# Attention with a mixture of experts on one core: a third buffer and a lead for converted weights, squares in a later place, an earlier column maximum, and row sums that VectorE adds up first

## The chip, the cores and the metric

The kernel runs on one core of one Trainium2 chip. The core has a matrix engine (TensorE, PE in the rows; PEld is its loading of weights), VectorE (DVE), ScalarE (ACT), GpSimd (POOL) and SyncE (SP), each with its own queue of instructions that it takes in order, and 16 DMA engines that all of them share. Engines wait for each other by semaphores. The metric is device time of one execution in microseconds (us).

## What is computed

```python
def _attn_ref(q, k, v, g_q, g_k):              # (4, 12, 448, 64) each
    def rmsnorm(x, g):
        rms = np.sqrt(np.mean(x * x, axis=-1, keepdims=True) + 1e-06)
        return x / rms * g
    q_n, k_n = (rmsnorm(q, g_q), rmsnorm(k, g_k))
    scores = scale * np.matmul(q_n, k_n.transpose(0, 1, 3, 2))
    scores = scores - np.max(scores, axis=-1, keepdims=True)
    attn = np.exp(scores)
    attn = attn / (np.sum(attn, axis=-1, keepdims=True) + 1e-09)
    return np.matmul(attn, v)

x = attention, as (1792, 768)                   # 4 batches of 448 tokens
x = np.maximum(x @ w_in, 0.0) ** 2 @ w_out      # 768 -> 2048 -> 768
logits = x @ phi                                # 32 slots of 8 experts
d = softmax(logits, axis 0); slot_input = d.T @ x
slot_out[e] = np.maximum(slot_input[e] @ w1[e], 0.0) @ w2[e]
out = softmax(logits, axis 1) @ slot_out
```

`w_in` and `w_out` come as 64-bit floats; the kernel turns them into 32-bit floats on the chip.

## The kernel before

The 48 heads are taken as 24 pairs (t = 0 to 23), six to a batch. `attention()` runs over t and, for each t, over the words of `ORDER`, a list written by hand that works on several pairs at once: loads for pair t+6, squares and roots for the norm of pair t+5, transposes of t+3, row maxima of t+2, scores, exponentials, values and sums of t, reciprocals of t-1, the finished pair of t-2. Between the words, a credit counter lets pieces of the expert input layer (`moe_hidden(b)`, for a batch whose six pairs are done) run on TensorE: 16 weight slices a batch, each 18 matmuls `ph<-xh,whl` (six row blocks, three products of high and low parts), then transposes of `gt` in groups of four slices. Up to t = 6 instructions keep the order of the code. Behind that a scheduler places them, by readiness and by their place in the code, so the built order of an engine is not the code's.

The weights reach the expert layer by *conversion units*, 16 of kind `in` and 16 of kind `out`. A unit is fetched (`fetch64`, a DMA of 768 KB that GpSimd issues into a buffer `w64`), then goes through `convert`: two steps on VectorE (`wf<-w`), three on ScalarE (`w<-w`, `wf<-wf`), a third on VectorE; an `in` unit is split and written to DRAM by GpSimd (`whl_s<-w`), from where SyncE loads it again as `whl`; an `out` unit is transposed on TensorE (`pm<-ident,wf`) and multiplied by phi. `CONVERT` says how many units each t starts, at the words `cvt`; `cvx` moves running units on. Units are fetched ahead by `prefetch`, into two buffers (`w64s`) once the expert layer has begun at t = 7, and `ensure` forces a unit that the expert layer needs at once.

What the steps of the argument touch: `square` (line 216: ScalarE squares a loaded `qk`, VectorE sums), `root` (230: at its end GpSimd multiplies four `qk` tiles), `scores` (291: the exponential `p<-pss` frees one of two PSUM buffers `pss`, which the next scores wait for), `values` and `fold` (305, 323), `sums` (327: four or eight matmuls with `ones`, then tiny DMAs `rsh<-sm`), `recip` (348: VectorE waits for `rsh`), `fetch64` to `ensure` (419 to 515), and `moe_hidden` and `dispatch` (545, 628). `dispatch` takes a batch's column maximum over `lsb`, exponentials `et`, and sums with `gn`. After batch 3 the attention's memory is released, and the weights of the eight experts (48 MB) stream in for the rest of the program.

Nearly all instructions are recorded in a helper, so that the rows have line 98 (100 after the change); the tiles tell them apart.

Of the kernel before, what the change touches and what calls it, by code (L numbers as in the profile page):

```python
# [17 lines left out]
def raw(ap):  # L18
# [6 lines left out]
ORDER = (  # L25
    "loadv load s0 mx0 row sq0 cvt out cvx s1 cvx mx1 v0 sq1 cvt cvx s2 cvx mx2 v1 recip cvt root0 cvx "
    "s3 cvx mx3 v2 cvt root1 cvx trans0 trans1 cvx v3 sum root2"
).split()
LEAD = 6

CONVERT = [0, 0, 0, 1, 0, 0, 1, 1, 2, 1, 2, 1, 2, 3, 3, 3, 3, 3, 3, 3]

PACE = 1.12
# [12 lines left out]
def tile_attention_moe_softmoe(  # L46
# [104 lines left out]
    state = {"h": ps_h, "m": ps_m, "n": 0, "cv": True, "w64": 0, "fc": -1, "h0": False, "held": 0}  # L151

# [23 lines left out]
    WF = 3  # L176
    PD = 3
    NSET = 3
# [126 lines left out]
    def values(t, c):  # L305
        if c == 0:
            live[t]["v"] = ps_v.tile([128, 512], F32, tag="v", name=name("pv"))
        ps = live[t]["v"]
        for j in range(2):
            for d in range(0, D, 32):  # L310
                g = 64 * j + d
                mm(
                    ps[g : g + 32, :S],
                    live[t]["vf"][:, j, c, d : d + 32],
                    live[t][f"p{c}"][:, j, :],
                    c == 0,
                    c == NC - 1,
                )
        if c % 2 and t >= FOLD:
            fold(t, c)  # L320


    def fold(t, c):
        p, p1 = live[t][f"p{c - 1}"], live[t][f"p{c}"]
        dve.tensor_tensor(p1, p1, p, ALU.add)

    def sums(t):
        ps = mps()
        folded = t >= FOLD
        for x in (1,) if folded else (0, 1):  # L330
# [5 lines left out]
        tt = att.tile([128, S], F32, tag="t", name=f"t_{t}", bufs=3)  # L336
        act.copy(tt, live[t]["v"][:, :S])
        live[t]["t"] = tt
        sm = att.tile([128, S], F32, tag="sm", name=f"sm_{t}", bufs=1)
        act.copy(sm, ps[:, :S])  # L340
        rsh = att.tile([32, 2, 28], F32, tag="rsh", name=f"rsh_{t}", bufs=2)
        for j in range(2):
            for i in range(2):
                g = 32 * (2 * j + i)
                sp.dma_start(rsh[16 * j : 16 * j + 16, i, :], sm[g : g + 1, :].rearrange("o (r e) -> o r e", r=16))
        live[t]["rsh"] = rsh

    def recip(t):
        rsh = live[t]["rsh"]
        rr = att.tile([32, 28], F32, tag="rr", name=f"rr_{t}", bufs=2)  # L350
        dve.scalar_tensor_tensor(rr, rsh[:, 0, :], TINY, rsh[:, 1, :], ALU.add, ALU.add)
        dve.reciprocal(rr, rr)
# [40 lines left out]

    def attention():
        for t in range(-LEAD, NT + 2):
            pin["on"] = t < PINNED
            todo = CONVERT[t + LEAD] if t + LEAD < len(CONVERT) else 0
# [85 lines left out]
    )  # L483
    fetched = {}
    running = []
# [7 lines left out]
    def convert_step(more, stages):  # L493
# [13 lines left out]
        if not (units or running):  # L507
            state["cv"] = False

    def convert_next():  # L510
# [34 lines left out]
    def moe_hidden(b):  # L545
# [40 lines left out]
        for fc in range(NFC):  # L586
# [39 lines left out]
        yield from dispatch(b, lsb, gn)  # L626

# [360 lines left out]
```

## Time and profile before

| | |
|---|---|
| Three runs, median (range) | 893.85 us (886.15 to 894.22) |
| The profiled execution: its time, and the span of its instructions | 893.53 us, 891.7 us |
| Busy: PE, PEld, DVE, ACT, POOL | 781.2, 471.7, 453.1, 358.9, 136.5 us |
| Mean granted TensorE clock | 0.946 of 2.4 GHz |
| DMA, mean over the span | 202 GB/s, 179.85 MB |

A row of a timeline has the start in us, the duration, engine, line, operation, out<-in, size and count, and in brackets how long the engine stood idle before it and what ended that. A row that counts several instructions has their joint duration. A row of a table by stretches has the stretch, its length, then for each engine busy us and count, the granted clock, the busy share of the DMA engines, and GB/s.

### The profile page before, as it was taken

The numbers are of one execution on the slowest core, as the hardware profiler recorded it, in microseconds if no ns is written. First come the engines' busy times: TensorE is split into PE (matmuls) and PEld (weight loads), VectorE is DVE, ScalarE is ACT, GpSimd is POOL, SyncE is SP. The second block draws the span as 40 slices with busy tenths as digits, with TensorE's granted clock in tenths as the row PEclk, the third lists the DMA queues.
The fourth block names the chain that finished last, engine by engine and source line by source line (L and its number), as shares of the span: only waits on it lengthen the run. The fifth ranks groups of instructions, "written<-read, shape, count | busy, mean of one in ns | idle before, by whom it ended". The sixth has DMA issues, their size and how long they took to land.

```text
span 891.7 us, 13289 instructions
## 1 busy us (share of the span) xinstructions
PE 781.2 (88%) x5162; PEld 471.7 (53%) x5162; DVE 453.1 (51%) x831; ACT 358.9 (40%) x564; POOL 136.5 (15%) x169
## 2 busy tenths in 40 slices
PE   0278888797997898999999999999999998988875
PEld 0134344464564655456666655666666885544433
DVE  4687878585575465456554665443126443210112
ACT  4347666663656354434333342342324432010101
POOL 3312322034142123003020100000000000000000
PEclk9999999699899797999999999999999999797895
DMA  8944667568767465524543421333336973899999
GB/s 268 248 130 143 204 195 214 150 208 290 215 229 255 169 215 173 200 88 124 153 131 109 140 93 47 128 107 113 118 117 245 359 292 136 318 401 348 348 348 295
DMA packets 122655, 179.85 MB, mean 202 GB/s; under 512 B 54624, under 2 KB 99168, under 8 KB 122592
## 3 DMA queue, kind: packets, MB, share of 16 engines
q1 hardware_dynamic: 112256, 129.45, 45.2%
q0 software_dynamic: 10336, 49.55, 16.1%
q8 instruction: 41, 0.67, 0.3%
q14 instruction: 22, 0.18, 0.1%
HBM read 148.73 MB, written 29.97 MB: 200 GB/s over the span
## 4 chain that ended last, share of the span: by engine, by line
PE 64%; DMA 10%; DVE 10%; issue 6%; ACT 5%; SPq 4%; POOL 1%; DVEq 0%; ACTq 0%; POOLq 0%
PE ph L98 23%; PE pm L98 14%; PE pss L98 9%; PE pv L98 7%; PE pe L98 4%; SPq L98 3%; DVE wf L98 3%; PE so_ps L98 3%; DVE nm L98 3%; DMA w<-in_moe_w_out_dram 2%; PE pt L98 2%; DMA w<-in_moe_w_in_dram 2%; DMA qk<-in_k_dram 2%; ACT w L98 1%; DMA w<-in_moe_w_dram 1%
## 5 line engine op out<-in xcount | busy, mean ns | idle before, releaser
L98 PE MATMUL ph<-xh,whl 128*128 128x448 f32 x1152 | 271.9, 379 | 0.7 <-ACT gt L98 0.7
L98 PEld LDWEIGHTS ph<-xh,whl 128*128 128x128 f32 x1152 | 208.2, 189 | 59.0 <-issue 30.2
L98 DVE TENSOR_REDUCE nm<-pss 112x2 f32<-112x896 f32 x96 | 104.2, 1086 | 73.4 <-PE pss L98 73.3
L98 ACT ACTIVATE p<-pss 112x896 f32<-112x896 f32 x96 | 87.9, 915 | 85.2 <-PE pss L98 84.1
L98 PE MATMUL pv<-p,vf 112*32 112x448 f32 x768 | 107.6, 566 | 0.0
L98 ACT ACTIVATE gt<-ph 128x448 f32<-128x448 f32 x64 | 34.8, 543 | 118.7 <-PE ph L98 112.6
L98 ACT ACTIVATE w<-w 128x768 int32<-128x768 f32 (+1 forms) x68 | 59.4, 879 | 36.7 <-DVE wf L98 34.3
L98 POOL TENSOR_TENSOR gt<-gt 128x448 f32<-128x448 f32 x33 | 31.1, 942 | 262.9 <-ACT gt L98 262.8
L98 POOL TENSOR_TENSOR qk<-qk,y 112x512 f32<-112x512 f32 x48 | 54.0, 1152 | 92.6 <-DVE y L98 63.8
L98 PE MATMUL pss<-qh,kh 64*112 64x448 f32 x192 | 46.3, 469 | 21.3 <-ACT p L98 18.5
L98 PE MATMUL pss<-kh,qh 64*112 64x448 f32 x192 | 44.4, 437 | 15.8 <-DVE nm L98 11.2
L98 PE MATMUL pm<-ident,qk 112*128 112x112 f32 x192 | 28.9, 290 | 31.9 <-POOL qk L98 31.0
L98 PEld LDWEIGHTS pss<-qh,kh 64*112 64x112 f32 x192 | 17.4, 175 | 65.0 <-ACT p L98 30.0
L98 PEld LDWEIGHTS pm<-ident,qk 112*128 112x128 f32 x192 | 23.2, 159 | 42.2 <-POOL qk L98 31.7
L98 DVE TENSOR_REDUCE ss<-sq 112x8 f32<-112x512 f32 x48 | 32.1, 674 | 22.1 <-ACT sq L98 21.8
L98 PE MATMUL pm<-ident,gt 128*112 128x128 f32 x256 | 40.9, 286 | 2.1 <-DVE ql L98 1.2
L98 PEld LDWEIGHTS pm<-ident,gt 128*112 128x112 f32 x256 | 28.3, 137 | 27.3 <-issue 14.1
L98 PE MATMUL pss<-ql,kh 64*112 64x448 f32 x192 | 41.5, 382 | 0.0
L98 PE MATMUL pss<-qh,kl 64*112 64x448 f32 x192 | 41.4, 382 | 0.0
L98 DVE SCALAR_TENSOR_TENSOR wf<-wf,w 128x768 f32<-128x768 f32 x32 | 31.9, 997 | 17.0 <-ACT w L98 11.5
L98 PE MATMUL pss<-mr,one 64*112 64x448 f32 x192 | 40.2, 377 | 0.0
L98 DVE TENSOR_TENSOR gt<-gt 128x448 f32<-128x448 f32 x22 | 13.9, 634 | 48.9 <-ACT gt L98 48.9
(145 smaller groups left out, 1010.2 us busy)
## 6 DMA issues: line engine op xcount, KB each, us to landing
w<-in_moe_w_dram SPq DMA_DIRECT2D x48, 1024.0 KB
whl<-whl_s SPq DMA_DIRECT2D x50, 768.0 KB
w<-in_moe_w_in_dram POOLq DMA_DIRECT2D x16, 768.0 KB, 6.5
w<-in_moe_w_out_dram POOLq DMA_DIRECT2D x16, 768.0 KB, 6.5
whl_s<-w POOLq DMA_DIRECT2D x16, 768.0 KB, 4.4
wo_s<-wf POOLq DMA_DIRECT2D x16, 384.0 KB, 6.4
wo<-wo_s SPq DMA_DIRECT2D x6, 1024.0 KB
qk<-in_q_dram SPq DMA_DIRECT2D x48, 112.0 KB
```

What stands on the lines that cost most here:

```text
L98: ins = f(*args, **kw)
```

## The change

1. *Conversion.* A third buffer `w64x`, used in turn with the two; four units ahead are fetched instead of three, three may be held instead of two. From t = 7 a unit starts only when its fetch was recorded at least `READY` = 4 calls of `convert_step` before, both `cvt` and `cvx` can start one, and what was not started stays on the account.
2. *Squares later.* In `ORDER`, `sq0` moves from behind `row` to behind the third scores, `sq1` from behind the first values to behind the fourth scores; `root0` moves ahead of the transposes and `root1` behind them.
3. *Maximum earlier.* In `moe_hidden`, the first part of `dispatch` (its maximum and exponentials) comes ahead of the last group's four transposes.
4. *Sums.* From pair 13 (`FOLD`), VectorE adds all four chunks of exponentials into the first (three adds, before two), and TensorE's four matmuls with `ones` have 224 columns each (before 448). The copy of the values `t` stands ahead of the sums.

```diff
-    "loadv load s0 mx0 row sq0 cvt out cvx s1 cvx mx1 v0 sq1 cvt cvx s2 cvx mx2 v1 recip cvt root0 cvx "
-    "s3 cvx mx3 v2 cvt root1 cvx trans0 trans1 cvx v3 sum root2"
+    "loadv load s0 mx0 row cvt out cvx s1 cvx mx1 v0 cvt cvx s2 cvx sq0 mx2 v1 recip cvt cvx "
+    "s3 cvx sq1 mx3 v2 cvt root0 cvx trans0 trans1 root1 cvx v3 sum root2"
+READY = 4
+    w64x = wst.tile([128, KC, 128, 2], I32, tag="w64x", name="w64x")
-    PD = 3
+    PD = 4
-        if c % 2 and t >= FOLD:
-            fold(t, c)
-    def fold(t, c):
-        p, p1 = live[t][f"p{c - 1}"], live[t][f"p{c}"]
-        dve.tensor_tensor(p1, p1, p, ALU.add)
+        if c and t >= FOLD:
+            p0 = live[t]["p0"]
+            dve.tensor_tensor(p0, p0, live[t][f"p{c}"], ALU.add)
...
-                    c = 2 * i + 1 if folded else 2 * x + i
-                    mm(ps[g : g + 32, :S], ones, live[t][f"p{c}"][:, j, :], folded or x == 0, x == 1)
+                    p = live[t]["p0"][:, j, i * HS : (i + 1) * HS] if folded else live[t][f"p{2 * x + i}"][:, j, :]
+                    mm(ps[g : g + 32, :w], ones, p, folded or x == 0, x == 1)
...
+            todo = max(todo, 0) + (CONVERT[t + LEAD] if t + LEAD < len(CONVERT) else 0)
-                        convert_step(key == "cvt" and todo > 0, 1 if pin["on"] else 2)
-                        todo -= key == "cvt"
+                        if pin["on"]:
+                            convert_step(key == "cvt" and todo > 0, 1)
+                            todo -= key == "cvt"
+                        else:
+                            todo -= convert_step(todo > 0, 2, READY)
...
-            w64 = w64s[state["w64"]]
-            state["w64"] ^= 1
+            w64 = w64s[state["w64"]] if state["w64"] < 2 else w64x
+            state["w64"] = (state["w64"] + 1) % 3
...
-            if key not in fetched and state["held"] < (2 if state["h0"] else 4):
+            if key not in fetched and state["held"] < (3 if state["h0"] else 4):
...
-        if more and units:
+        begin = more and units and not (ready and state["tick"] - since.get(units[0], state["tick"]) < ready)
+        if begin:
...
-        for c in pend:
-            yield c
+        yield next(pend)
+        rest = dispatch(b, lsb, gn)
+        yield next(rest)
+        yield from pend
```

Three places of the built orders follow, before and after. First ScalarE in pair 6: `p_6_1` is the exponential of the pair's second chunk, `sq_12_0` the square of pair 12's q tile. Before:

```order
L98 ACTIVATE p_6_0_1449<-pss_135_1440 112x896
L98 ACTIVATE sq_11_0_1462<-qk_11_0_1255 112x512
L98 ACTIVATE wf_118_1290<-wf_118_1290 128x768
L98 ACTIVATE p_6_1_1480<-pss_139_1471 112x896
L98 ACTIVATE sq_11_1_1491<-qk_11_1_1258 112x512
L98 CAST xh_0_1669<-xf_4_1469 128x448
L98 ACTIVATE sq_12_0_1655<-qk_12_0_1434 112x512
L98 ACTIVATE p_6_2_1508<-pss_144_1499 112x896
L98 ACTIVATE sq_12_1_1768<-qk_12_1_1437 112x512
```

and after:

```order
L100 COPY sm_6_1603<-pm_154_1600 128x448
L100 ACTIVATE w64_131_1394<-w64_131_1394 128x768
L100 ACTIVATE p_7_1_1731<-pss_164_1722 112x896
L100 ACTIVATE sq_12_0_1822<-qk_12_0_1435 112x512
L100 CAST xh_0_1666<-xf_5_1664 128x448
L100 COPY wt_160_1707<-pm_161_1708 128x512
L100 ACTIVATE sq_12_1_1885<-qk_12_1_1438 112x512
```

The squares of pair 12 moved from ahead of the third exponential of pair 6 to behind the second one of pair 7.

Second GpSimd around the four multiplies `qk_12_0` to `qk_13_1`; a `DMA w64..<-in_moe_w` is the fetch of a unit, `whl_s` the write of a split one. Before:

```order
L98 DMA wi_s_90<-wf_191_2019 128x768
L98 DMA whl_s_91<-w64_1_94 128x1536
L98 TENSOR_TENSOR qk_12_0_1434<-qk_12_0_1434,y_13_2149 112x512
L98 TENSOR_TENSOR qk_12_1_1437<-qk_12_1_1437,y_13_2149 112x512
L98 TENSOR_TENSOR qk_13_0_1626<-qk_13_0_1626,y_13_2149 112x512
L98 TENSOR_TENSOR qk_13_1_1629<-qk_13_1_1629,y_13_2149 112x512
L98 DMA w64_1_94<-in_moe_w_in_dram 128x6x256
L98 TENSOR_TENSOR gt_3_1995<-gt_3_1995 128x448
L98 DMA w64_0_93<-in_moe_w_out_dram 128x1536
```

and after:

```order
L100 DMA w64_0_93<-in_moe_w_in_dram 128x6x256
L100 DMA wo_s_92<-wf_174_1819 128x768
L100 TENSOR_TENSOR gt_2_1927<-gt_2_1927 128x448
L100 DMA wi_s_90<-wf_191_2018 128x768
L100 DMA whl_s_91<-w64_1_94 128x1536
L100 DMA w64x_110<-in_moe_w_in_dram 128x6x256
L100 TENSOR_TENSOR gt_3_1997<-gt_3_1997 128x448
L100 DMA w64_1_94<-in_moe_w_out_dram 128x1536
L100 DMA wo_s_92<-wf_192_2024 128x768
L100 DMA whl_s_91<-w64_0_93 128x1536
L100 TENSOR_TENSOR gt_4_2099<-gt_4_2099 128x448
L100 DMA wi_s_90<-wf_194_2042 128x768
```

Unit in 9 is the `w64_1` fetch before and the `w64_0` fetch after. Its fetch, and those of in 10 and out 9, moved from behind the four multiplies to ahead of them; after the change the multiplies follow the last row shown.

Third GpSimd at the start of the program, up to the first multiply `qk_0_0`, which the first transposes on TensorE wait for. Before:

```order
L98 DMA w64_0_93<-in_moe_w_out_dram 128x1536
L98 DMA w64_1_94<-in_moe_w_in_dram 128x6x256
L98 DMA whl_s_91<-w64_1_160 128x1536
L98 DMA w64_6_178<-in_moe_w_out_dram 128x1536
L98 DMA w64_7_180<-in_moe_w_in_dram 128x6x256
L98 DMA whl_s_91<-w64_2_162 128x1536
L98 TENSOR_TENSOR qk_0_0_147<-qk_0_0_147,y_1_210 112x512
```

and after:

```order
L100 DMA w64_4_167<-in_moe_w_out_dram 128x1536
L100 DMA w64_0_93<-in_moe_w_out_dram 128x1536
L100 DMA w64_1_94<-in_moe_w_in_dram 128x6x256
L100 DMA whl_s_91<-w64_1_161 128x1536
L100 DMA w64x_110<-in_moe_w_out_dram 128x1536
L100 DMA w64_7_181<-in_moe_w_in_dram 128x6x256
L100 DMA whl_s_91<-w64_2_163 128x1536
L100 DMA w64_8_191<-in_moe_w_out_dram 128x1536
L100 TENSOR_TENSOR qk_0_0_148<-qk_0_0_148,y_1_213 112x512
```

Two more fetches, `w64x` and `w64_8`, now stand ahead of the first multiply; `w64_7` and `w64_8` take the buffers that the two `whl_s` writes read.

## Rows read from the trace of the kernel before

**Rows 1.** Page, 40 equal slices of 22.3 us: busy tenths of TensorE and VectorE

```profile
PE   0278888797997898999999999999999998988875
DVE  4687878585575465456554665443126443210112
```

**Rows 2.** Table by stretches: length, busy us (count) per engine, clock, DMA share, GB/s

```profile
0.00:25.00 25.00, 0.00 (x0) 0.00 (x0) 11.12 (x28) 9.66 (x13) 8.41 (x18) 1.00 0.91 269
...
150.00:175.00 25.00, 18.58 (x105) 10.71 (x107) 15.34 (x31) 14.97 (x23) 2.17 (x4) 0.73 0.52 158
...
200.00:225.00 25.00, 18.38 (x118) 11.97 (x118) 13.84 (x25) 11.19 (x18) 9.62 (x11) 0.93 0.81 280
225.00:250.00 25.00, 23.85 (x157) 14.40 (x155) 13.87 (x20) 16.33 (x25) 5.30 (x8) 0.94 0.67 202
...
275.00:300.00 25.00, 18.91 (x110) 12.57 (x109) 13.89 (x22) 12.91 (x20) 2.47 (x4) 0.80 0.58 191
284.00:292.00 8.00, 2.89 (x20) 1.93 (x19) 3.64 (x8) 2.79 (x4) 0.42 (x1) 0.85 0.98 341
...
325.00:350.00 25.00, 22.41 (x119) 12.25 (x115) 18.42 (x35) 13.04 (x20) 9.12 (x11) 0.88 0.54 171
350.00:375.00 25.00, 23.55 (x121) 12.69 (x122) 10.57 (x17) 10.02 (x15) 2.55 (x4) 0.84 0.60 213
```

**Rows 3.** Timeline of TensorE, the first row behind each of four stops

```profile
161.73 0.71 PE L98 MATMUL pss<-qh,kh 64*112 64x448 f32 x2 [5.00 <-ACT p L98]
...
223.95 0.71 PE L98 MATMUL pss<-qh,kh 64*112 64x448 f32 x2 [6.62 <-ACT p L98]
...
292.07 0.69 PE L98 MATMUL pm<-ident,wf 128*128 128x128 f32 x2 [4.66 <-DVE gn L98]
...
344.67 0.71 PE L98 MATMUL pss<-qh,kh 64*112 64x448 f32 x2 [2.58 <-DVE nm L98]
```

**Rows 4.** Timelines of ScalarE and VectorE, what they waited for at these stops

```profile
160.25 0.63 ACT L98 ACTIVATE sq<-qk 112x512 f32<-112x512 f32 x1 [6.12 <-DMA qk<-in_q_dram]
...
220.62 0.56 DVE L98 TENSOR_SCALAR wf<-w 128x768 int32<-128x768 int32 x1 [6.63 <-DMA w<-in_moe_w_in_dram]
...
288.12 0.56 DVE L98 TENSOR_SCALAR wf<-w 128x768 int32<-128x768 int32 x1 [2.85 <-DMA w<-in_moe_w_in_dram]
290.19 0.18 DVE L98 SCALAR_TENSOR_TENSOR rr<-rsh 32x28 f32<-32x28 f32 x1 [1.51 <-DMA rsh<-sm]
...
337.89 2.61 DVE L98 TENSOR_SCALAR wf<-w 128x768 int32<-128x768 int32 x2 [1.25 <-DMA w<-in_moe_w_out_dram]
```

**Rows 5.** Waits of VectorE, 150 to 380 us: total, times, longest

```profile
DVE wf L98 <- DMA w<-in_moe_w_in_dram: 14.7, 4, 6.6
```

**Rows 6.** Chain that ended last: ten score matmuls at the low and the full clock

```profile
161.73 2.21 PE pss L98 x10
...
174.38 1.20 PE pss L98 x10
```

**Rows 7.** Timeline of GpSimd ahead of the second stop

```profile
207.01 4.76 POOL L98 TENSOR_TENSOR qk<-qk,y 112x512 f32<-112x512 f32 x4 [3.36 <-issue]
211.72 0.90 POOL L98 DMA_DIRECT2D w<-in_moe_w_in_dram  x1
```

**Rows 8.** Timeline of GpSimd at the start

```profile
22.50 0.84 POOL L98 DMA_DIRECT2D w<-in_moe_w_in_dram  x1 [6.18 <-DMA whl_s<-w]
...
29.09 5.77 POOL L98 TENSOR_TENSOR qk<-qk,y 112x512 f32<-112x512 f32 x4 [5.21 <-issue]
```

**Rows 9.** Page, DMA issues: KB each, median us to landing

```profile
whl_s<-w POOLq DMA_DIRECT2D x16, 768.0 KB, 4.4
```

**Rows 10.** The sums: TensorE's timeline, and VectorE's group, 430 to 680 us

```profile
146.60 1.69 PE L98 MATMUL pm<-p,ones 112*32 112x448 f32 x16
...
L98 DVE TENSOR_TENSOR p<-p,p 112x896 f32<-112x896 f32 x20 | 22.3, 1116 | 23.8 <-PE pv L98 19.5 <-ACT p L98 4.2
```

**Rows 11.** Timeline of TensorE at the end of the expert input layer

```profile
755.07 0.40 PE L98 MATMUL pm<-ident,et 32*112 32x32 f32 x4 [2.15 <-ACT et L98]
```

More of the change, by code (lines that the diff above doesn't have):

```diff
@@ L150, in tile_attention_moe_softmoe @@
     ps_s = tc.alloc_tile_pool(name="ps_s", bufs=2, space=PSUM)
-    state = {"h": ps_h, "m": ps_m, "n": 0, "cv": True, "w64": 0, "fc": -1, "h0": False, "held": 0}
+    state = {"h": ps_h, "m": ps_m, "n": 0, "cv": True, "w64": 0, "fc": -1, "h0": False, "held": 0, "tick": 0}
     def name(s):
@@ L318, in values @@
                 )
-        if c % 2 and t >= FOLD:
-            fold(t, c)
-    def fold(t, c):
-        p, p1 = live[t][f"p{c - 1}"], live[t][f"p{c}"]
-        dve.tensor_tensor(p1, p1, p, ALU.add)
+        if c and t >= FOLD:
+            p0 = live[t]["p0"]
+            dve.tensor_tensor(p0, p0, live[t][f"p{c}"], ALU.add)
+    HS = S // 2
     def sums(t):
@@ L329, in sums @@
         folded = t >= FOLD
+        tt = att.tile([128, S], F32, tag="t", name=f"t_{t}", bufs=3)
+        act.copy(tt, live[t]["v"][:, :S])
+        live[t]["t"] = tt
+        sm = att.tile([128, S], F32, tag="sm", name=f"sm_{t}", bufs=1)
+        rsh = att.tile([32, 2, 28], F32, tag="rsh", name=f"rsh_{t}", bufs=2)
+        live[t]["rsh"] = rsh
+        w = HS if folded else S
         for x in (1,) if folded else (0, 1):
@@ L333, in sums @@
                     g = 32 * (2 * j + i)
-                    c = 2 * i + 1 if folded else 2 * x + i
-                    mm(ps[g : g + 32, :S], ones, live[t][f"p{c}"][:, j, :], folded or x == 0, x == 1)
[L336 to L341, printed above, removed]
+                    p = live[t]["p0"][:, j, i * HS : (i + 1) * HS] if folded else live[t][f"p{2 * x + i}"][:, j, :]
+                    mm(ps[g : g + 32, :w], ones, p, folded or x == 0, x == 1)
+        act.copy(sm[:, :w], ps[:, :w])
         for j in range(2):
@@ L344, in sums @@
                 g = 32 * (2 * j + i)
-                sp.dma_start(rsh[16 * j : 16 * j + 16, i, :], sm[g : g + 1, :].rearrange("o (r e) -> o r e", r=16))
-        live[t]["rsh"] = rsh
+                r = slice(16 * j + 8 * i, 16 * j + 8 * i + 8) if folded else slice(16 * j, 16 * j + 16)
+                src = sm[g : g + 1, :w].rearrange("o (r e) -> o r e", e=28)
+                sp.dma_start(rsh[r, 0 if folded else i, :], src)
     def recip(t):
@@ L350, in recip @@
         rr = att.tile([32, 28], F32, tag="rr", name=f"rr_{t}", bufs=2)
-        dve.scalar_tensor_tensor(rr, rsh[:, 0, :], TINY, rsh[:, 1, :], ALU.add, ALU.add)
+        if t >= FOLD:
+            dve.tensor_scalar(rr, rsh[:, 0, :], TINY, None, ALU.add)
+        else:
+            dve.scalar_tensor_tensor(rr, rsh[:, 0, :], TINY, rsh[:, 1, :], ALU.add, ALU.add)
         dve.reciprocal(rr, rr)
@@ L394, in attention @@
     def attention():
+        todo = 0
         for t in range(-LEAD, NT + 2):
             pin["on"] = t < PINNED
-            todo = CONVERT[t + LEAD] if t + LEAD < len(CONVERT) else 0
+            todo = max(todo, 0) + (CONVERT[t + LEAD] if t + LEAD < len(CONVERT) else 0)
             for key in ORDER:
@@ L400, in attention @@
                     if key == "cvt" or state["h0"]:
-                        convert_step(key == "cvt" and todo > 0, 1 if pin["on"] else 2)
-                        todo -= key == "cvt"
+                        if pin["on"]:
+                            convert_step(key == "cvt" and todo > 0, 1)
+                            todo -= key == "cvt"
+                        else:
+                            todo -= convert_step(todo > 0, 2, READY)
                     continue
@@ L484, in tile_attention_moe_softmoe @@
     fetched = {}
+    since = {}
     running = []
@@ L488, in prefetch, with convert_step @@
         for key in units[:PD]:
-            if key not in fetched and state["held"] < (2 if state["h0"] else 4):
+            if key not in fetched and state["held"] < (3 if state["h0"] else 4):
                 state["held"] += 1
                 fetched[key] = fetch64(*key)
-    def convert_step(more, stages):
+                since[key] = state["tick"]
+    def convert_step(more, stages, ready=0):
+        state["tick"] += 1
+        if ready:
+            prefetch()
         for unit in list(running):
@@ L508, in convert_step @@
             state["cv"] = False
+        return bool(begin)
     def convert_next():
@@ L625, in moe_hidden @@
             state["fc"] += 1
-        yield from dispatch(b, lsb, gn)
+        yield from rest
     def dispatch(b, lsb, gn):
```

## The prediction

> **What bounds the kernel now.** I read the page's slices first. From slice 16 on (about 355 us) to slice 32 TensorE is at 9 tenths or more; before that it is at 7 to 9, with holes [rows 1]. So from 355 us on the time is TensorE's work, and waiting can only be gained back ahead of that, in the tail, or by giving TensorE less to do. The table by stretches shows where the early time goes: between 150 and 375 us TensorE loses 6.4 us of one 25 us stretch, 6.6 of another, 6.1 of a third, and in the same stretches the granted clock is 0.73, 0.93 and 0.80 instead of 1.00 [rows 2]. TensorE's timeline then names four stops: 5.00, 6.62, 4.66 and 2.58 us, together 18.9 us [rows 3]. Behind each the clock is at its lower level of 1.2 GHz for a while. A clock of 0.73 over 25 us means 2 x 0.27 x 25 = 13.5 us at that level; the same sum gives 3.5 and 3.0 us for 200 to 250, 10.0 for 275 to 300, and 6.0 and 8.0 for 325 to 375 [rows 2].
>
> What stood behind the stops is on the other engines [rows 4]. First stop: ScalarE came to a square whose `qk` load was still under way and waited 6.12 us, with the exponential that frees the scores' PSUM buffer queued behind it. Second: VectorE waited 6.63 us for a fetched unit, and ScalarE's next step and exponential came after that. Third: VectorE waited 2.85 us for a unit and 1.51 us for `rsh`, and its `gn` copy, which frees a PSUM buffer, stood behind. Fourth: VectorE waited for a unit again, and the two first steps took 2.61 us. Over 150 to 380 us VectorE's waits for `in` units alone are 14.7 us [rows 5].
>
> **The sum, part by part.** It is made against the profiled execution, 893.53 us (span 891.7); the median of the runs is 893.85, so the two are the same for this purpose.
>
> *Price of the lower clock.* Ten score matmuls take 2.21 us at the low level and 1.20 at the full one [rows 6], so a stretch at the low level wastes 46% of its length if TensorE alone sets the pace. It does not quite: in 150 to 175 us ScalarE is busy 14.97 and VectorE 15.34 of 25 us [rows 2], and with TensorE twice as fast they would have to follow. I take half, 23%; the bounds are 0 and 46%.
>
> *Squares later.* ScalarE's order shows pair 12's squares behind the second exponential of pair 7, almost a whole pair after their load. The first stop goes: 5.0 us, and 23% of its 13.5 us, 3.1. That is 8.1 us (bounds 0 and 11.2). The squares themselves are not fewer. At 0, the stop comes back at another square: the scheduler now puts pair 15's squares ahead of pair 9's first exponential, where they stood behind it.
>
> *Third buffer and lead.* Stops two to four are 6.62 + 4.66 + 2.58 = 13.9 us, their low-clock time 3.5 + 3.0 + 10.0 + 14.0 = 30.5 us, of which 23% is 7.0; in all 20.9 (27.9 at the upper price). How much goes? Before, unit in 9 is fetched behind four multiplies that start at 207.01 and take 4.76 us; the fetch comes at 211.72 and VectorE has it at 220.62 [rows 4, 7]. GpSimd's new order has this fetch and two more ahead of the multiplies. Issued at 207 instead of 211.7 it would be 4.7 us earlier and leave 6.63 - 4.71 = 1.9 us of the wait; the 2.85 and 1.25 us waits are shorter than 4.7 and would go [rows 4]. Against that, the scheduler also begins units earlier: VectorE's order has five, not four, begun between the row maxima of pairs 9 and 10, so part of the lead is spent. And the 1.51 us for `rsh` is not a unit's. I take two thirds of 20.9, **13.9 us**; bounds 0 and 27.9, and below 0 in a rival. The `READY` rule issues nothing.
>
> *Sums.* Sixteen sum instructions take 1.69 us [rows 10], 0.106 each. From pair 13 a pair has eight, 0.85 us; at half the columns 0.42. Eleven pairs save 11 x 0.42 = 4.7 us of TensorE, where it is full; bounds 0 (if loading the `ones` sets the pace) and 4.7. VectorE gets eleven more adds at 1.116 us, 12.3 us, in a part where it is at 3 to 6 tenths [rows 1, 10]; this idle time hides them, and without it they would cost up to 12.3. The last add reads the fourth chunk and no longer writes it, so it need not wait for the value matmuls, which the adds now wait 19.5 us for in twenty [rows 10]; the sums come no later.
>
> *Maximum earlier.* At the end TensorE waits 2.15 us for `et` [rows 11]. The maximum and exponential now run beside the last group's transposes: 2.0 us (bounds 0 and 2.15). For batches 0 to 2 other matmuls hid it.
>
> *Start.* Two more fetches stand ahead of the first multiply. `w64_8` needs the buffer that the second `whl_s` write reads. That write is issued at about 23.3, behind the fetch at 22.50; with 4.4 us to land (median) `w64_8` goes out near 28, and with the 6.2 us that the first write was waited for, near 29.5; half a microsecond later come the multiplies, which began at 29.09 [rows 8, 9]. So 0 to 1 us from the queue. DMA moves 269 GB/s at a share of 0.91 in these 25 us [rows 2], so one more 768 KB, of `w64x`, is up to 2.9 us for the loads beside it. I take **2.0 us** lost; bounds 0 and 3.9.
>
> *End of batch 0.* TensorE's order has the last two weight slices of batch 0 in pair 11's stretch, where they stood in pair 12's, but conversions are ahead by only about one unit. Their way is a `whl_s` write (4.4 us) [rows 9] and a load back; TensorE would stand at `ph` with everything behind it. I take **3 us** lost (less than one write); bounds 0 and 10 (two units, a landing and a half each). The copy of `t` ahead of the sums and the other moved roots I cost at 0: GpSimd's multiplies are needed only near the end of the next pair.
>
> Sum: 893.5 - 8.1 - 13.9 - 4.7 - 2.0 + 2.0 + 3.0 = 869.8, **870 us**. TensorE is the bound up to the tail, so an early gain is kept; the experts' weights begin to load when attention ends, and that moves along.
>
> **The rivals.**
>
> *All stops go* (13 in 100): the upper bounds, 893.5 - 11.2 - 27.9 - 4.7 - 2.1 + 2.0 = 850 us. For it: no wait for an `in` unit is longer than 6.6 us [rows 5], and passing the multiplies alone gives 4.7. Against: `rsh`.
>
> *The lead is spent* (20 in 100): the change doesn't do what it says, because the scheduler, which does not know how late a load lands, starts units as early as it can. Then the third term is 0: 893.5 - 8.1 - 4.7 - 2.0 + 5.0 = 884 us. For it: the fifth unit above.
>
> *Nor do the squares help* (12 in 100): ScalarE meets pair 15's load instead. Then 893.5 - 4.7 - 2.0 + 5.0 = 892 us.
>
> *Slower: loads crowd each other* (8 in 100). Three fetches outstanding are 2.3 MB. In the third stop DMA was at a share of 0.98 [rows 2], and `rsh`, tiny, came late by 1.51 us [rows 4]. If 17 units in six bursts of three each cost one stop like the third (4.66 + 2.3 = 7.0 us), that is 42 instead of 20.9: 893.5 + 21.1 - 8.1 - 4.7 - 2.0 + 5.0 = 905 us. It takes six such stops to be slower by over 1%; against it speaks that the mean share in these stretches is only 0.5 to 0.8 [rows 2], so the bytes fit.
>
> The Trainium skill, DMA: Bandwidth & Descriptors, section Issuing engines are not separate DMA queues, speaks for this rival: transfers of all issuing engines run on the same 16 DMA engines and interleave, so a fetch issued earlier takes its time from the loads beside it. At the start the trace agrees (share 0.91 and 269 GB/s); by that rule alone the start would cost its full 2.9 us, and the sum would be 871.
>
> **How the numbers follow.** The main case has 47 in 100 and alone spans 860 to 880 (half or five sixths of the 20.9, the start at its bounds). The range leaves out the slower case, about half of the case at 892 and a little of the lowest: 852 to 891. A measurement of this kernel can tell about 1% from no change, so faster means below 885: 47 + 13 + 11 of the 20 = 71. Slower (above 903) is 8. The rest, 21, is the same.
>
> **What would show it.** Squares: no wait for `qk` above 1 us ahead of an exponential in pairs 6 and 7, and a clock of 1.00 there. Buffer: VectorE's waits for `in` units at 5 us or below, and at most two stops of TensorE above 2 us between 150 and 400 us. Sums: eight instructions of 224 columns at about half the time. Start: first multiplies between 29 and 33 us. Batch 0: no wait of `ph` for `whl`. The prediction is wrong if units' waits stay near 14 us, if a new stop above 4 us stands at a square or at `ph`, or if TensorE is no longer full between pairs 12 and 13, where the new order has little expert work.

## The result, and the profile after

| | before | after |
|---|---|---|
| Median (range) of five runs each, side by side | 893.85 us (886.15 to 894.92) | 882.6 us (875.75 to 884.69) |
| Ratio, 95% interval | | 0.9891 (0.9848 to 0.9934) |
| The profiled execution: time, span | 893.53, 891.7 us | 875.75, 873.7 us |
| Busy: PE, DVE, ACT, POOL | 781.2, 453.1, 358.9, 136.5 us | 762.7, 472.6, 357.9, 141.5 us |

The change makes the kernel 1.1% faster, 9.7 us by the ratio; 870 us, a gain of 24 us, was forecast, in a range of 852 to 891 us that holds the time. Ratios in this text leave out runs in a second, slower state that some executions show, and are not quite the quotients of the medians (here 0.9874). The profiled execution of after is the fastest of its five, 7 us below their median, so the difference of the two profiles (18 us) shows more gain than there is.

The waits ahead of 400 us have changed their owner. First the rows of after that answer to [rows 3], the first row behind each stop of TensorE of 2 us or more between 150 and 400 us:

```profile
195.27 0.92 PE L100 MATMUL pm<-ident,wf 128*128 128x128 f32 x6 [2.37 <-DVE wf L100]
...
221.78 1.53 PE L100 MATMUL pm<-phi_sb,wt 128*128 128x32 f32 x12 [3.39 <-ACT wt L100]
...
247.19 0.71 PE L100 MATMUL pss<-qh,kh 64*112 64x448 f32 x2 [2.00 <-ACT p L100]
...
285.18 1.10 PE L100 MATMUL pm<-ident,gt 128*112 128x128 f32 x4 [2.86 <-ACT sm L100]
...
326.21 1.10 PE L100 MATMUL pm<-ident,gt 128*112 128x128 f32 x4 [4.33 <-ACT sm L100]
```

The long stops of 5.00 and 6.62 us are gone, but there are five of 2.0 to 4.3 us, 15.0 us where [rows 3] add up to 18.9. Next VectorE's waits for units, as in [rows 5], and ScalarE's waits of squares for loads, both over 150 to 380 us (total, times, longest):

```profile
DVE wf L100 <- DMA w<-in_moe_w_in_dram: 6.3, 1, 6.3
```

```profile
ACT sq L100 <- DMA qk<-in_q_dram: 14.6, 3, 6.5
```

VectorE's wait for `in` units fell from 14.7 to 6.3 us. ScalarE's for q was 6.6 us before (two times, the 6.12 us of [rows 4] among them) and is 14.6 now, as three others. ScalarE's timeline shows what the longest holds up:

```profile
315.31 0.53 ACT L100 COPY t<-pv 128x448 f32<-128x448 f32 x1 [1.30 <-PE pv L100]
322.39 0.63 ACT L100 ACTIVATE sq<-qk 112x512 f32<-112x512 f32 x1 [6.54 <-DMA qk<-in_q_dram]
...
325.64 0.52 ACT L100 COPY sm<-pm 128x448 f32<-128x448 f32 x1
```

and SyncE's and the table by stretches show the load that it waits for:

```profile
312.22 1.35 SPq L100 DMA_DIRECT2D qk<-in_q_dram  x2
```

```profile
272.80:283.10 10.30, 9.52 (x64) 5.82 (x63) 3.12 (x5) 3.92 (x7) 1.64 (x3) 1.00 0.98 319
312.90:322.40 9.50, 8.17 (x61) 4.22 (x59) 2.49 (x4) 1.18 (x3) 1.38 (x3) 1.00 0.99 308
```

The square of pair 17's q stands right behind its load, waits 6.54 us for it, and the copy `sm`, which frees the PSUM buffer that TensorE waits 4.33 us for, comes behind. From the issue of the load to the square pass some 10 us, in which the DMA engines are busy at a share of 0.99; pair 16's load, in the other stretch, is the same. In before the square of pair 17's q started as late after its load, 10.0 us behind the issue at 316.35. But there it stood behind `sm` and behind the exponential; ScalarE had other work until then and did not wait:

```profile
325.57 0.95 ACT L98 ACTIVATE p<-pss 112x896 f32<-112x896 f32 x1
326.37 1.20 ACT L98 ACTIVATE sq<-qk 112x512 f32<-112x512 f32 x2
```

The clock over the whole stretch is what it was; here 100 to 400 us before and after (the count behind TensorE's busy time is its matmuls):

```profile
100.00:400.00 300.00, 266.97 (x1684) 158.69 (x1683) 190.42 (x335) 167.10 (x250) 72.24 (x95) 0.93 0.61 199
```

```profile
100.00:400.00 300.00, 267.74 (x1740) 163.44 (x1740) 205.84 (x363) 172.30 (x256) 80.31 (x99) 0.93 0.62 199
```

A clock of 0.93 over 300 us is 42 us at the lower level, in both.

The other terms went nearly as forecast. The start: GpSimd's first multiplies begin at 32.43 us, behind the wait of a fetch; before they began at 29.09 [rows 8].

```profile
31.88 0.53 POOL L100 DMA_DIRECT2D w<-in_moe_w_out_dram  x1 [6.94 <-DMA whl_s<-w]
32.43 4.15 POOL L100 TENSOR_TENSOR qk<-qk,y 112x512 f32<-112x512 f32 x4
```

The sums: eight instructions take 0.96 us before (first row, of the kernel before) and 0.59 us after.

```profile
443.59 0.96 PE L98 MATMUL pm<-p,ones 112*32 112x448 f32 x8
```

```profile
434.61 0.59 PE L100 MATMUL pm<-p,ones 112*32 112x224 f32 x8
```

The end of the expert layer, TensorE's waits over 700 to 760 us: 0.4 us for `et` where [rows 11] had 2.15. And batch 0's weights, over 25 to 400 us:

```profile
PE pm L100 <- ACT et L100: 0.4, 1, 0.4
```

```profile
PE ph L100 <- DMA whl<-whl_s: 1.2, 1, 1.2
```

### The profile page after: what moved, and what is told of

It reads as the page before. It is cut to its first block, busy times and chain, and to the rows that moved or that the text cites. A ratio compares the mean times of both kernels' runs of the same rounds, so it can differ in the third digit from the quotient of the medians.

```text
span 873.7 us, 13333 instructions
## 1 busy us (share of the span) xinstructions
PE 762.7 (87%) x5162; PEld 470.2 (54%) x5162; DVE 472.6 (54%) x842; ACT 357.9 (41%) x564; POOL 141.5 (16%) x169
## 4 chain that ended last, share of the span: by engine, by line
PE 61%; DMA 10%; DVE 9%; issue 7%; ACT 5%; SPq 4%; POOL 2%; DVEq 0%; ACTq 0%; POOLq 0%
PE ph L100 23%; PE pm L100 13%; PE pss L100 9%; PE pv L100 7%; PE pe L100 4%; SPq L100 3%; DMA qk<-in_k_dram 3%; DMA w<-in_moe_w_dram 3%; DVE wf L100 2%; DVE nm L100 2%; PE pt L100 2%; DMA wo_s<-wf 2%; PE so_ps L100 2%; DMA whl_s<-w 1%; ACT p L100 1%
## 5 line engine op out<-in xcount | busy, mean ns | idle before, releaser
L100 PE MATMUL pv<-p,vf 112*32 112x448 f32 x768 | 101.7, 556 | 0.0
L100 POOL TENSOR_TENSOR gt<-gt 128x448 f32<-128x448 f32 x33 | 34.5, 1047 | 249.5 <-ACT gt L100 249.5
L100 PE MATMUL pss<-kh,qh 64*112 64x448 f32 x192 | 42.5, 434 | 18.2 <-DVE nm L100 16.8
L100 PE MATMUL pm<-ident,qk 112*128 112x112 f32 x192 | 28.3, 285 | 34.3 <-POOL qk L100 33.6
L100 ACT ACTIVATE w<-w 128x768 int32<-128x768 f32 (+2 forms) x58 | 50.2, 868 | 17.4 <-DVE wf L100 15.1
L100 DVE TENSOR_TENSOR p<-p,p 112x896 f32<-112x896 f32 x33 | 38.9, 1177 | 18.0 <-ACT p L100 12.7
L100 ACT ACTIVATE sq<-qk 112x512 f32<-112x512 f32 x48 | 30.0, 628 | 32.2 <-DMA qk<-in_q_dram 24.0
L100 PE MATMUL pss<-qh,kl 64*112 64x448 f32 x192 | 39.3, 381 | 0.0
L100 PEld LDWEIGHTS pss<-kh,qh 64*112 64x112 f32 x192 | 18.4, 183 | 37.9 <-DVE nm L100 24.4
```

The costliest lines, as they stand in the source:

```text
L100: ins = f(*args, **kw)
```

## The experiments

All ratios are to the kernel before, run on the same chip beside them; "us" is that ratio times the median of before there.

| run | what it is | ratio (95%) | us |
|---|---|---|---|
| e1 | before + conversion part | 1.0048 (1.0010 to 1.0086) | +4.3 |
| e2 | before + squares later | 0.9938 (0.9909 to 0.9967) | -5.5 |
| e3 | before + sums | 0.9929 (0.9894 to 0.9964) | -6.3 |
| e4 | before + maximum earlier | 0.9955 (0.9923 to 0.9987) | -4.0 |
| e5 | after without conversion part | 0.9847 (0.9823 to 0.9871) | -13.6 |
| e6 | after, three units of lead up to t = 7 | 0.9939 (0.9907 to 0.9971) | -5.4 |
| e7 | after, q and k loaded a pair earlier | 0.9932 (0.9901 to 0.9962) | -6.1 |
| e8 | e5, q and k loaded a pair earlier | 0.9870 (0.9835 to 0.9905) | -11.6 |
| e9 | after, squares kept in place | 0.9802 (0.9765 to 0.9840) | -17.7 |
| e10 | e5, squares kept | 0.9880 (0.9845 to 0.9914) | -10.7 |
| e11 | e5 + third buffer without lead | 0.9834 (0.9803 to 0.9864) | -14.8 |
| e12 | after, READY = 0 | 0.9883 (0.9855 to 0.9911) | -10.4 |
| e13 | e1, squares kept | 0.9812 (0.9770 to 0.9854) | -16.7 |
| e14 | before, squares kept | 0.9959 (0.9923 to 0.9995) | -3.6 |
| e15 | e11, squares kept | 0.9828 (0.9784 to 0.9873) | -15.3 |
| e16 | e9, three units of lead up to t = 7 | 0.9820 (0.9776 to 0.9864) | -16.0 |
| e17 | after, squares at their old places and kept | 0.9699 (0.9661 to 0.9737) | -26.8 |
| e18 | e17, three units of lead up to t = 7 | 0.9669 (0.9634 to 0.9703) | -29.5 |

### One part at a time

Each of the first four kernels has one numbered part of the diff above and nothing else. Cut to a few lines each:

```diff
 # e1
+    w64x = wst.tile([128, KC, 128, 2], I32, tag="w64x", name="w64x")
-    PD = 3
+    PD = 4
 # e2: the two lines of ORDER
 # e3: sums, recip, and the adds in values
 # e4
+        rest = dispatch(b, lsb, gn)
+        yield next(rest)
```

> Before, with the conversion's part of the change alone: third buffer, four units of lead, the READY rule, the carry-over of units not begun. The squares, the sums and the maximum stay as before. Theory 'the lead is spent' (the missing gain is this part's): TensorE still stops at units begun too early and the start costs 2 to 3 us, so the time is that of before, -2 to +4 us. Rival 'the buffer helps as predicted, something else spoilt it': 8.9 to 13.9 us faster (13.9 less the 5 us that start and end of batch 0 were priced at). Rival 'loads crowd': 10 us slower or more. In the trace, theory: VectorE's waits for fetched units between 150 and 380 us stay over 8 us, or other waits of the same sum take their place; rival: they fall to 6 us and TensorE's time of waiting ahead of 400 us falls by 10 us or more.

> Before, with the new places of the squares and roots alone. Theory 'the squares help as priced': 8.1 us faster, the stop of 5.0 us near 162 us gone and no other in its place. Rival 'the squares are put behind their loads again': the order that is built places the squares of pairs 14 to 17 just behind their loads, ScalarE waits for these, and the gain is 0 to 3 us; then ScalarE's waits of squares for qk over the whole attention are above 12 us, where before has 6.6.

> Before, with the sums of one chunk alone (from pair 13 on three adds per pair, sums over 224 columns, the copy of t ahead of the sums). Theory: TensorE does 11 x 0.42 = 4.7 us less from pair 13 on, where it is full, so 4.7 us faster. Rival 'the loads of the ones set the pace or the adds come late': 0 to 2 us. Rival 'VectorE's adds are on the path': up to 12 us slower.

> Before, with the maximum ahead of the last transposes alone. Theory: the 2.15 us in which TensorE waits for et at the end go, 2.0 us faster. Rival 'the experts' weights set the end, not et': 0 us, since the tail waits for loads of weights that are not issued earlier. Rival 'the maximum comes ahead of other work of VectorE in batches 0 to 2 and delays it': 2 us slower.

The four add up to -11.5 us, and the whole change is at -9.7 (-13.6 to -5.9), so the parts hardly disturb each other. Three of them gain what they should, within their intervals. The conversion part costs 4.3 us where 8.9 were to be gained: the missing gain is all there. Its trace has the waits of after, and larger; the profiled execution, 905.50 us, is the longest of its twelve (median 897.0), so a usual run may have less of them. VectorE's wait for `in` units and ScalarE's waits of squares for q, 150 to 380 us:

```profile
DVE wf L100 <- DMA w<-in_moe_w_in_dram: 4.7, 1, 4.7
```

```profile
ACT sq L100 <- DMA qk<-in_q_dram: 28.6, 5, 10.8
```

and its longest stop, in ScalarE's, TensorE's and SyncE's timeline and the table by stretches:

```profile
260.02 0.63 ACT L100 ACTIVATE sq<-qk 112x512 f32<-112x512 f32 x1 [10.81 <-DMA qk<-in_q_dram]
...
261.95 0.90 ACT L100 ACTIVATE p<-pss 112x896 f32<-112x896 f32 x1
```

```profile
262.90 0.72 PE L100 MATMUL pss<-qh,kh 64*112 64x448 f32 x2 [8.74 <-ACT p L100]
```

```profile
246.48 0.60 SPq L100 DMA_DIRECT2D qk<-in_q_dram  x1
```

```profile
246.50:260.00 13.50, 7.66 (x52) 4.84 (x50) 1.72 (x3) 2.68 (x5) 1.91 (x3) 0.94 0.95 297
```

The units are there in time, as forecast (14.7 us of waits to 4.7). But the load of pair 15's q, issued at 246.48, is waited for until 260.02, 13.5 us, with the DMA engines at 0.95; GpSimd issued three fetches of 768 KB from 245.07 to 251.75. ScalarE has the square ahead of pair 9's first exponential and stands 10.81 us, TensorE 8.74. In before it stood behind that exponential, began 10.0 us after its load was issued (250.89 and 240.90), and did not wait. So "the lead is spent" is wrong in its mechanism (the waits for units went), and "the buffer helps" is wrong in its sum.

### Without the part, and with an earlier load

e5 is after with the conversion of before. e6 changes one line of after, e7 four (and `t` to two buffers, for room), e8 makes e7's four in e5:

```diff
 # e6
-        for key in units[:PD]:
+        for key in units[: PD if state["h0"] else 3]:
 # e7, e8
-LEAD = 6
+LEAD = 7
-CONVERT = [0, 0, 0, 1,
+CONVERT = [0, 0, 0, 0, 1,
-        "load": (6, 0, lambda t: load(t)),
+        "load": (7, 0, lambda t: load(t)),
-            x = att.tile([CP, NC, 2, D], F32, tag="qk", name=f"qk_{t}_{i}", bufs=8)
+            x = att.tile([CP, NC, 2, D], F32, tag="qk", name=f"qk_{t}_{i}", bufs=10)
```

> After, with the conversion as before (two buffers, three units of lead, no READY): squares, sums and maximum as changed. Theory 'the conversion's part costs what it costs alone, and the parts add up': the three gains measured alone (5.5, 6.3 and 4.0 us) remain, 15.8 us faster than before, a ratio of 0.982, and 4 to 6 us faster than the whole change. Rival 'the lead pays once the squares stand later': the whole change is as fast or faster than this one, a ratio of 0.989 or above.

> After, with three units of lead as before until the first batch's experts begin, and four from there. The third buffer's first fetch no longer stands ahead of the first multiplies. Theory 'the start's loss is kept to the end': first multiplies at 31 us again where the whole change has 33.6, and 2.6 us faster than the whole change, a ratio to before of 0.986. Rival 'TensorE makes it up while it waits anyway': first multiplies at 31, the same time as the whole change, 0.989.

> After, with the loads of q and k issued one pair earlier, into 10 buffers where there were 8 (and 2 buffers of t for 3, to make room). Theory 'the fetches of the longer lead and the loads of whl on SP's queue make the loads of q and k late, ScalarE stands at squares and TensorE's gain is lost there': ScalarE's waits of squares for qk between 25 and 400 us fall from 21 us to below 6, and the time is 5 to 9 us below the whole change, a ratio of 0.979 to 0.984. Rival 'these waits of ScalarE are beside the path': the waits fall and the time stays, 0.987 to 0.991. Rival 'fetches crowd each other and whatever comes with them': another load's wait (mr, rsh, rb, whl) takes their place, 0.989 or above.

> After without the conversion's part, and with the loads of q and k one pair earlier, into 10 buffers. Theory 'late loads of q and k hold ScalarE even without the longer lead': 2 to 5 us faster than the same kernel with loads as they were, a ratio of 0.977 to 0.980. Rival 'without the longer lead no square waits on the path': the same as that kernel, 0.982, or slower by the start (one more pair of loads, 448 KB, ahead of the rest: 1 to 2 us).

e5 came out near the theory: 13.6 us of the expected 15.8, 4 us better than the whole change. The theories of the other three missed; e8 is 2.0 us slower than e5, as its rival had it. In e6 GpSimd's first multiplies begin at 31.29 us, 1.1 earlier than after, and the time is no better, so the start alone isn't it.

e5 also has the one load that can be compared like for like. The square of pair 16's q stands ahead of pair 10's first exponential in before, after, e1, e2 and e5. First the load and the square in e5, then the same in after with GpSimd's fetches beside them, then both stretches from load to square:

```profile
271.17 2.01 SPq L98 DMA_DIRECT2D qk<-in_q_dram  x2
...
276.70 0.63 ACT L98 ACTIVATE sq<-qk 112x512 f32<-112x512 f32 x1 [1.66 <-DMA qk<-in_q_dram]
```

```profile
271.10 0.97 POOL L100 DMA_DIRECT2D w<-in_moe_w_in_dram  x1
...
272.15 1.48 SPq L100 DMA_DIRECT2D qk<-in_q_dram  x2
...
272.84 0.55 POOL L100 DMA_DIRECT2D w64x<-in_moe_w_out_dram  x1 [0.76 <-DMA whl_s<-w64x]
...
283.10 0.63 ACT L100 ACTIVATE sq<-qk 112x512 f32<-112x512 f32 x1 [4.72 <-DMA qk<-in_q_dram]
```

```profile
271.20:276.70 5.50, 5.50 (x39) 3.84 (x37) 3.33 (x5) 1.70 (x4) 0.48 (x2) 0.90 0.79 227
272.20:283.10 10.90, 10.12 (x65) 5.82 (x63) 3.72 (x6) 4.36 (x8) 1.64 (x3) 1.00 0.98 322
```

Without the longer lead GpSimd issues no fetch between 262.37 and 276.35 (one `whl_s` write, at 270.79), and the load is there after 5.5 us (5.6 in e2); with it, two fetches go out within 2 us around the load, and it is waited for until 10.9 us after its issue (11.9 in e1).

e7 was meant to settle the matter and did not, and the reason is worth a look. ScalarE's waits for q over 150 to 380 us fell to 8.3 us only:

```profile
ACT sq L100 <- DMA qk<-in_q_dram: 8.3, 3, 4.3
```

With the loads a pair earlier the scheduler put the squares a pair earlier too: pair 15's q is loaded at 210.80 us and squared at 223.71, behind the first exponential of pair 8; in after 236.84 and 244.54, ahead of the first of pair 9. So ten buffers gave less slack than a pair. The second part of the change had not settled their places either: it moved the squares of pairs up to 13, while for pairs 15 and 17 the traces show them behind the first exponential of pairs 9 and 11 in before, e2 and e5, and ahead of it in after, e1, e11 and e12, all of which have the third buffer. So the next step was to hold the squares.

### Keeping the squares in their place

The edit is one line: it ties each square, at all pairs, behind the ScalarE instruction that precedes it in the code, as all instructions are up to t = 6.

```diff
 # e9, e10, e13 to e18
-        act.activation(sq, live[t]["qk"][i].rearrange("p c h d -> p (c h) d"), AF.Square)
+        tc.keep_in_program_order(act.activation(sq, live[t]["qk"][i].rearrange("p c h d -> p (c h) d"), AF.Square))
 # e11, e15: in e5, w64x and its turn; PD = 3, two held
+            w64 = w64s[state["w64"]] if state["w64"] < 2 else w64x
+            state["w64"] = (state["w64"] + 1) % 3
 # e12
-READY = 4
+READY = 0
```

> After, with each square kept behind the ScalarE instruction that stands before it in the code, also from pair 7 on, where the scheduler has put the squares of pairs 14 to 17 ahead of the first exponentials of pairs 9 to 11, right behind their loads. Nothing else changes. Theory 'the longer lead makes loads of q land 3 us later, and the scheduler's squares wait for them on the path': ScalarE's waits of squares for qk between 150 and 380 us (14.9 us in the whole change) go below 2 us, and the time falls to that of the change without its conversion part or below it, a ratio of 0.975 to 0.985. Rival 'the conversion part costs elsewhere (start, clock, bursts on the DMA engines)': the waits go and the time stays at 0.989 to 0.994.

> After without the conversion's part (0.9847 before), with each square kept behind the ScalarE instruction before it in the code. Without the longer lead squares wait only 2.0 us for qk in 150 to 380 us. Theory: as there is nearly no wait to remove, the same time, 0.982 to 0.987. Rival 'late squares delay the roots and GpSimd's multiplies, and so the transposes': slower, 0.990 or above.

> After without the conversion's part, but with the third buffer in turn with the two; still three units of lead and two held, so no more fetches under way at a time, and no READY. Theory 'the cost lies in the lead, not in the buffer': 0.982 to 0.987, as without the part. Rival 'the buffer does what was forecast, since a fetch no longer waits for the write that reads its buffer': 3 us faster or more, 0.981 or below. Rival 'the buffer alone costs': 0.989 or above.

> After with READY = 0: third buffer and four units of lead stay, but a unit starts as soon as its turn comes, however young its fetch. Theory 'the lead's fetches crowd the loads of q': as the whole change or a little slower, 0.989 to 0.995, with VectorE's waits for units up again from 8.5 us to 14 us or more. Rival 'READY's hold makes units late for the experts of batch 0 and dense behind it': faster than the whole change, 0.985 or below.

e9 is at 872.84 us, 0.9802: with the squares kept, the whole change is near the 870 us that was forecast. No square waits for a load between 150 and 380 us in its trace. Without the conversion part the same edit gives nothing or costs (e10, 0.9880, against 0.9847), so it is the two together: with kept squares the part is worth 7.0 us (e9 against e10, same chip). e12, without READY and without the `prefetch` that `convert_step` makes only where READY is set, is as fast as after (0.9883; waits for `in` units 5.7 us against 6.3, not the rise that was expected).

e11 has the time of its theory, the cost lies in the lead, but does not fit cleanly. With the third buffer and no longer lead its squares wait as long as in after:

```profile
ACT sq L98 <- DMA qk<-in_q_dram: 15.1, 4, 6.6
```

and yet it is at 0.9834, below the whole change, though the two intervals touch. And in e12 ScalarE waits 8.1 us for q, not 14.6, at the time of after. So the sum of ScalarE's waits isn't the price by itself. That it matters which of them falls on a moment when TensorE has other work is likely; no run shows it.

### The conversion part alone, with kept squares

> Before with the conversion's part alone (that was 1.0048), and each square kept behind the ScalarE instruction before it in the code, at the old places in the code. Theory 'the conversion part saves what was forecast as soon as squares do not stand right behind their loads': 6 to 9 us less than before with the kept squares alone, and so a ratio of 0.980 to 0.988. Rival 'the conversion part costs 4 us wherever squares stand, and keeping them only helps by itself': 4 us more than before with the kept squares alone, 0.995 to 1.000.

> Before, with nothing but each square kept behind the ScalarE instruction before it in the code. In the built order pair 12's squares move from the end of pair 6 to pair 7, past the 6.12 us wait for their load; those of pairs 14 to 17 move a pair later. Theory: the first stop of TensorE (5.0 us and its low clock) goes, the waits for fetched units stay, 3 to 6 us faster, 0.993 to 0.997, so most of the gain in the kernel with lead and kept squares is not the keeping's own. Rival 'the keeping is the gain itself': 0.985 or below.

> After with kept squares (0.9802), but only the third buffer of the conversion's part: three units of lead, two held, no READY. Theory 'the buffer gives most of what the conversion part gives, the lead the smaller rest': 0.978 to 0.983. Rival 'it is the lead and READY that pay': as without the conversion's part and with kept squares, 0.986 to 0.990.

> After with kept squares (0.9802), and three units of lead until the first batch's experts begin. Theory 'with the squares out of the way TensorE keeps what the start gives back': first multiplies 1 us earlier (32.6 for 33.7, as in the whole change with that start), and 1 us faster, 0.979. Rival 'TensorE waits for the loads of the first pairs all the same': 0.980 to 0.984.

The first pair shows where the loss lies. On the same chip, before with kept squares has a median of 883.64 us and the conversion part on top of it 869.65, 14.0 us less (13.1 by the two ratios); where the squares stand free the same part costs 4.3. The table by stretches, 100 to 400 us, first of e14, then of e13:

```profile
100.00:400.00 300.00, 269.09 (x1734) 161.14 (x1731) 192.42 (x343) 169.98 (x253) 72.70 (x96) 0.95 0.64 201
```

```profile
100.00:400.00 300.00, 275.00 (x1867) 166.82 (x1860) 202.50 (x367) 177.92 (x268) 77.13 (x97) 0.97 0.66 210
```

e13 does 133 matmuls more in these 300 us, at a clock of 0.97; TensorE is idle for 25.0 us of them instead of 30.9. Its loads are issued as early as after's, but no square stands right behind them: pair 15's q is issued at 236.60 and squared at 276.23.

```profile
236.60 0.64 SPq L100 DMA_DIRECT2D qk<-in_q_dram  x1
```

```profile
276.23 1.14 ACT L100 ACTIVATE sq<-qk 112x512 f32<-112x512 f32 x2
```

One thing was not as expected: VectorE's waits for `in` units are down to 6.3 us in e2 and 3.0 in e14 without any lead (14.7 in before), so part of those waits had been a consequence of ScalarE's order. With those for `out` units they are 18.7 us in before, 13.9 in e2, and 6.6 in both e14 and e13. So with kept squares the part takes nothing off the waits that it was made for, and the 14 us of e13 are not that row; which wait they come from, no run shows.

e15 and e16 lie within the interval of e9, so buffer against lead, and start, are not told apart by them.

### The version the runs point to

Conversion part and kept squares gave 0.9812 without the squares' new places, the sums or the maximum; the whole change with kept squares 0.9802. Either the gains overlap, or the new places, once the squares are really held there, take something back.

```diff
 # e17: after with the kept squares, and before's ORDER; e18: also e6's line
-    "loadv load s0 mx0 row cvt out cvx s1 cvx mx1 v0 cvt cvx s2 cvx sq0 mx2 v1 recip cvt cvx "
+    "loadv load s0 mx0 row sq0 cvt out cvx s1 cvx mx1 v0 sq1 cvt cvx s2 cvx mx2 v1 recip cvt root0 cvx "
...
```

> After with each square kept behind the ScalarE instruction before it in the code, but at the places in the code that squares and roots had before: so conversion part, sums and maximum of the change without its second part. Theory 'parts add up, and the new places of the squares bring nothing once they are kept': conversion part with kept squares 0.9812, sums alone 6.3 us, maximum alone 4.0 us, together 16.7 + 6.3 + 4.0 = 27 us less, a ratio of 0.967 to 0.973. Rival 'the gains overlap, as at the new places, where all with kept squares is 0.9802 only': 0.977 to 0.983.

> The same with three units of lead until the first batch's experts begin. Theory: first multiplies 1 us earlier and the time the same or 1 us less, 0.966 to 0.973. Rival 'fewer units ahead at the change of the rule': 2 us more.

The parts add up: 26.8 us of the expected 27. e18, at a median of 861.56 us, is 3.3% faster than before, and beats after, at 0.9891, by 2.2%; it is 2.7 us below e17, with intervals that overlap. Its slices of TensorE and of the clock:

```profile
PE   0179788899799999999999999999999998988865
PEclk9999999999799989999999999999999999887985
```

TensorE is full from slice 11 on, about 236 us, where in before it is from slice 16 [rows 1]. The new places of the squares gained 5.5 us alone; where squares are held they cost some 9 us (e9 against e17, with intervals that don't overlap). That late squares then make the roots and GpSimd's multiplies late is the likely way; no run shows it.

## Why the prediction was wrong

| term | forecast | measured alone (95%) |
|---|---|---|
| squares later | -8.1 | -5.5 (-8.1 to -2.9) |
| third buffer, lead, start, end of batch 0 | -13.9 + 2.0 + 3.0 = -8.9 | +4.3 (+0.9 to +7.7) |
| sums | -4.7 | -6.3 (-9.5 to -3.2) |
| maximum earlier | -2.0 | -4.0 (-6.9 to -1.2) |
| all | -23.7 | -9.7 (-13.6 to -5.9) |

**Third buffer and lead.** This is the step that failed, and in it one sentence: "I take two thirds of 20.9, 13.9 us". The step read [rows 4, 5, 7] rightly as far as they went: the fetches did come earlier, and VectorE's waits for `in` units fell from 14.7 to 4.7 us with the part alone. But it booked a wait that goes as time that goes, and did not ask what shares the DMA engines with a fetch that is issued earlier and who stands ready to wait for that. Those were the loads of q of pairs 15 to 17, and the squares right behind them. Two things met there: at pairs 15 and 17 the squares were now placed ahead of the exponential that they had followed, and pair 16's load, whose square kept its place, landed 5 us later (10.9 us for 5.5). Both halves were in the text: that pair 15's squares move ahead of pair 9's first exponential stands under *Squares later*, and that loads crowd each other is a rival with 8 in 100. They were never put together; the rival named `rsh` as the load that comes late, not q. The stop of 4.33 us behind a square is one of the signs that the prediction itself named for being wrong. Runs e13 and e14 show what the part is worth with the squares held: 13 to 14 us net, more than the 8.9 forecast. That does not confirm the forecast's way, since the waits for units that it priced are 6.6 us in both; where the 14 us come from stays open.

The Trainium skill, DMA: Bandwidth & Descriptors, section Issuing engines are not separate DMA queues, says that transfers started by ScalarE, SyncE or GpSimd run on the same 16 DMA engines and interleave. By that rule SyncE's load of q can be slowed by GpSimd's fetches, and the traces of pair 16 agree: 10.9 us from issue to square at a share of 0.98 with two fetches beside it, 5.5 us at 0.79 without. The prediction named the rule for its slower rival and priced it at the start only.

**Which rival came.** The measured time is that of "the lead is spent" (884), by another way: the lead was not spent on earlier units but paid back at other loads. That the number fits is luck.

**Squares later.** The first stop went and no square waits for q in pairs 6 and 7. The clock from 150 to 175 us rose from 0.73 to 0.93, not to 1.00:

```profile
150.00:175.00 25.00, 22.85 (x171) 11.25 (x163) 19.79 (x40) 19.55 (x29) 3.55 (x6) 0.93 0.66 195
```

The size lies at the edge of the interval. "At most two stops above 2 us" was wrong, and the 10.1 us that were put on the clock in both terms together did not come: with the long stops gone and shorter ones there, the mean clock of 100 to 400 us is 0.93 as before.

**Sums and maximum.** Right in mechanism and within the intervals. The sums' instruction is halved in columns and takes 0.61 of the time, not half (0.59 us of 0.96), so TensorE gets 11 x 0.37 = 4.1 us of the 4.7; no cost of the adds shows in e3's time. The maximum takes 1.75 us off the wait for `et`; its interval allows that.

**Start and end of batch 0.** First multiplies at 32.43, within 29 to 33, TensorE's first wait 33.6 us for 31.0: 2.6 us for 2.0. `ph` waits 1.2 us for `whl` where 3 were priced.

**Left open.** Why e11 is faster than after with equal waits of ScalarE, and e12 is not with fewer; which wait the 14 us come from, and how much of them is buffer and how much lead; and how much of ScalarE's waiting is the squares' earlier place and how much the later landing, since holding the squares removes both. SyncE, which issues the load, also waits over 100 to 400 us for `whl_s` writes, with other loads queued behind; but that is 19.6 us in before and 20.2 in e1, and pair 16's lateness counts from the issue.

## What to carry to other kernels

A transfer that is issued earlier can take its time from the transfers beside it, so before a wait is booked as a gain, list the small loads that are under way in the same microseconds and the first instruction that stands behind each. Where a scheduler places instructions without knowing when a load lands, more buffers or an earlier load may only let it place the consumer earlier; here the slack came from tying the consumer to a late place. And test the parts of a change one at a time: here four parts hid a loss of 4 us under gains of 16, and that part became the largest gain with one line.

## What the runs showed of the hardware

A load of q (two transfers of 112 KB) was waited for until 13.5 us after its issue with the DMA engines at a share of 0.95 and 297 GB/s (pair 15, e1), 10.9 us at 0.98 (pair 16, after) and 5.5 us at 0.79 (pair 16, e5); in before the square of pair 13's q came 3.35 us behind its load and did not wait. I had expected the big fetches to suffer from crowding, not the small loads. The fetches of `in` units took longer too, but by less: a median of 6.5 us to landing in before and 7.7 in after, over 150 to 380 us.

TensorE's mean granted clock of 100 to 400 us did not follow the longest stops: 0.93 with stops of 5.00 and 6.62 us (before), 0.93 with none above 4.33 (after), and 0.97 in e13, which has one stop above 2 us there, of 5.75.
